# A fused attention and feed-forward kernel: another order of work up to the first MLP stage, quad 5's normalisation by a float32 product, and a planner that counts transfers as they run

## The chip, the cores and the metric

The kernel runs on one core of a Trainium2 chip. TensorE (PE) multiplies matrices into PSUM, which has eight banks; VectorE (DVE), ScalarE (ACT) and GpSimd (POOL) work on 128 partitions of SBUF; SyncE (SP) computes nothing and issues DMA transfers. SP, ACT and POOL each have a DMA queue of their own. Each engine runs its instructions in the order in which they were written for it, and waits on semaphores for the others. The metric is the device time of one execution in microseconds, lower is better.

## What is computed

Cosine attention over 8 batches of 12 heads, 448 positions and 64 dimensions, followed by a two-layer MLP over the 3584 tokens:

```python
q_n = q / (np.linalg.norm(q, axis=-1, keepdims=True) + 1e-06)
k_n = k / (np.linalg.norm(k, axis=-1, keepdims=True) + 1e-06)
scores = np.matmul(q_n, k_n.transpose(0, 1, 3, 2)) / tau          # tau = 0.1
attn = np.exp(scores - np.max(scores, axis=-1, keepdims=True))
attn = attn / (np.sum(attn, axis=-1, keepdims=True) + 1e-09)
x = np.matmul(attn, v).transpose(0, 2, 1, 3).reshape(3584, 768)
h = x @ w_in                                                      # 768 x 2048
out = (h * np.cos(h)) @ w_out                                     # 2048 x 768
```

## The kernel before

**Quads.** Attention runs over 24 quads of four heads each (three to a batch), and each quad over seven steps of 64 keys per head. Q and K are loaded in float32 (`load_one`, L398), squared (`square`, L448 and L450), summed (L454), turned into reciprocal norms (`inverse`, L480 to L493: logarithm and exponential on ACT, and for quads 1 to `FAST` = 7 a VectorE sum and reciprocal in place of the last two ACT steps) and scaled to bfloat16 (`scale`, L501). Then they are transposed: by PE for the first four quads (`transpose`, L523 and the copy at L534), by a transposing DMA on SP after that (`turn`, L544). A step's `scores` (L560) go to PSUM, one ACT exponential (L567) writes E, and `attend` (L577) adds E times V into banks 4 and 5.

**Sums and normalisation.** For quads 0 to 2 the sums of the exponentials are spread over all partitions by a product with ones (`spread`, L602) and inverted on ACT (L611, L612). From quad 3 on, `sums` (L645) makes them for one or two quads in one round with a narrow selector matrix: ACT inverts them (L652, L654) into Zs, SP writes Zs to a scratch tensor in DRAM (L655), two SP loads for each quad read it back spread over 64 partitions each (R, L661), and GpSimd (VectorE for quad 5) multiplies the saved product of E and V by R into xT (L665). Rounds before are [3], [4, 5], [6, 7] and so on.

**MLP.** For each batch c, 16 blocks of the first layer (`m1_part`, L679, 6 products each) run in 8 pairs, followed by ACT and VectorE steps for h cos h (`m1`, L697 to L703). The second layer (`m2`, L715) runs in tiles of 128 tokens and halves of 384 columns, 16 products each; VectorE copies a half out (L733) and SP stores it (L739). The first layer of batch 1 needs quads 3, 4 and 5, that of batch 2 needs quads 6, 7 and 8, and so on. W1 comes in four and W2 in four transfers on GpSimd's queue (L420, L425), V on the same queue (L410).

**Order.** Quads 0 to 2 are written out by hand, and under `P.strict` ACT, VectorE and GpSimd keep that order. Behind them a loop over the batches interleaves: while the second layer of batch c runs, quads of later batches do their scores and attend steps (five quads in c = 0: 3 to 7; then four, three, three, three, three). `group` writes two steps and `fill` the second-layer products between them; it also places the rounds that are due. PE always keeps the written order. For the other engines `Planner.pass_` simulates the program with booked durations and takes, for each engine, the ready operation with the earliest due time (`prio`: the time by which its reader on PE needs it, less a `lead`). `land` books DMA transfers: 1.2 us to the first byte, `moves` us of transfer, lengthened where another queue is active, 0.8 us to the semaphore:

```python
s = max(issued + self.FIRST, self.ring[ring])
...
self.ring[ring] = s + took
return self.ring[ring] + self.LAST
```

`warm` runs products on an identity matrix to keep PE busy at the start. Zs has two buffers, R two, the Q and K loads three each, V four.

Of the kernel before, what the change touches and what calls it, by code (L numbers as in the profile page):

```python
# [21 lines left out]
class Planner:  # L22
# [10 lines left out]
    FIRST, LAST = 1.2, 0.8  # L33
# [36 lines left out]
    def land(self, ring, issued, took):  # L70

        s = max(issued + self.FIRST, self.ring[ring])
        alone = took
        for other in self.ring:
            if other != ring:
                both = min(took, max(0.0, self.ring[other] - s))
                took += both
                if both:
                    self.ring[other] += min(both, alone)
        self.ring[ring] = s + took  # L80
        return self.ring[ring] + self.LAST

    PASSES, SPREAD = 0, 1.5

    def plan(self):

        rng = random.Random(1)
        shift = [0.0] * len(self.ops)
        least = max(o.end for o in self.pass_(shift))
        for _ in range(self.PASSES):  # L90
            n = rng.choice((8, 30, 100))
            i = rng.randrange(len(shift) - n)
            tried = list(shift)
            for k in range(i, i + n):
                tried[k] += rng.gauss(0.0, self.SPREAD)
            end = max(o.end for o in self.pass_(tried))
            if end <= least:
                least, shift = end, tried
        self.order = self.pass_(shift)
        return self.order  # L100

    def pass_(self, shift):
# [38 lines left out]
        self.ring = {"sp": 0.0, "pool": 0.0, "act": 0.0}  # L141
# [4 lines left out]
        while len(done) < len(ops):  # L146
            best = None
            for e in self.ENGINES:
# [16 lines left out]
                if best is None or s < best[0]:  # L165
                    best = (s, e, c)
            s, e, c = best
# [10 lines left out]
            o.end = self.land(e, avail[e], o.moves) if o.dma else s + o.dur + o.lat  # L178
            done.append(o)
            if c in queue:  # L180
                u = queue[c]
                left[u] -= 1
                if not left[u]:
                    pending[e].append(u)
            for u in users[c]:
# [86 lines left out]
def bass_cosine_attention__then__act_gcu_kernel(  # L272
# [49 lines left out]
    Zs = ring("Zs", 2, [128, S], F32)  # L322
# [34 lines left out]
    op("dve", 0.1, lambda e: e.memset(zeros, 0.0), w=["zeros", "iot"])  # L357

# [34 lines left out]
    def load_one(qd, w, part=ALL[0], after=(), eng="sp"):  # L393
# [5 lines left out]
                  w=cut(nm, s, part), dma=(nm, s, j0), moves=0.157 * (j1 - j0), after=after, keep=qd > 4)  # L399
# [7 lines left out]
    def load_v(qd, after=()):  # L407
# [3 lines left out]
                  w=[("V", s)], dma=("V", s), moves=1.34, after=after)  # L411
# [11 lines left out]
    def load_w2(i, hf):  # L423
        src = moe_w_out.rearrange("(f p) n -> p f n", p=128)[:, 8 * i:8 * i + 8, HW * hf:HW * hf + HW]
        return pool_dma(0.79, lambda e: e.dma_start(W2.ap()[:, 8 * i:8 * i + 8, HW * hf:HW * hf + HW], src),  # L425
                 w=[("W2", i, hf)], dma=("W2", i, hf), moves=4.14)

    H, NLEAD, FAST = 2 * NJ, 5.0, 7
# [110 lines left out]
    def turn(qd):  # L539
# [3 lines left out]
        for n, t, nm in ((Qn, qT, "Q"), (Kn, kT, "K")):  # L543
            turned[qd].append(op("sp", 1.3, lambda e, n=n, t=t: e.dma_start_transpose(  # L544
                t[u].ap().rearrange("p j a x -> p j (a x)"), n[u].ap().rearrange("p j r d -> p (j r d)")),
               r=cut(nm + "n", u, ALL[0]), w=cut(nm + "T", u, ALL[0]), dma=(nm + "T", u), moves=1.29, keep=True))
# [41 lines left out]
    Z, LEAD = 6, 15.0  # L588
# [44 lines left out]
    def sums(quads, bk):  # L633
# [3 lines left out]
        z = n % 2  # L637
# [17 lines left out]
        op("sp", 0.5, lambda e: e.dma_start(rscr.ap()[8 * n:8 * n + rows, :], Zs[z].ap()[0:32 * np_:16, :]),  # L655
           r=[("Zs", z)], w=[("rs", n)], dma=("rs", z), moves=0.05, lead=LEAD)
        for i, qd in enumerate(quads):
            u, sl, b = qd % 2, qd % NA, qd // QB
            for r in range(2):
                ap = bass.AP(rscr, (8 * n + 4 * i + 2 * r) * S, [[0, 64], [S, 2], [1, S]])  # L660
                op("sp", 0.5, lambda e, r=r, u=u, ap=ap: e.dma_start(R[u].ap()[64 * r:64 * r + 64], ap),  # L661
                   r=[("rs", n)], w=[("R", u, r)], after=spared, dma=("R", u, r), moves=0.68, lead=LEAD)
            c0 = 2 * (qd % QB)
            late = qd == 2 * QB - 1
            op("dve" if late else "pool", 1.02 if late else 2.04, lambda e, u=u, sl=sl, b=b, c0=c0: e.tensor_tensor(  # L665
                xT[b % 2].ap()[:, c0:c0 + 2, :], AVs[sl].ap(), R[u].ap(), ALU.mult),
                r=[("AV", sl), ("R", u, 0), ("R", u, 1)], w=[("x", b % 2, qd % QB)], lead=LEAD)

# [40 lines left out]
    def m2(t, h, f0, f1, bk):  # L709
# [11 lines left out]
        if f1 == NNB and t == B * S // 128 - 1:  # L721
# [3 lines left out]
            for sg, eng in enumerate(("sp", "act" if h else "sp")):  # L725
# [4 lines left out]
                   r=[("o", so, h)], w=[("out", t, sg, h)], dma=("store", t, h, sg), moves=0.26)  # L730
# [82 lines left out]
    for _ in key:  # L813
        pass
# [226 lines left out]
```

## Time and profile before

| | us |
|---|---|
| median of 3 runs (lowest, highest) | 438.72 (436.95, 439.27) |
| the profiled execution's own time | 440.37 |
| its span | 438.6 |
| first exponential of quad 0 starts | 12.32 |
| first layer of batch 0 starts (L679) | 37.09 |
| quads 3 to 7 with the second layer of batch 0 | 60.30 to 95.95 |
| first layer of batch 1 starts | 98.72 |
| mean granted PE clock | 0.995 |

The span is the time between the first and the last instruction of one profiled execution; the time of that execution has another 1.8 us around it. A line of the profile's timeline gives start, duration, engine, source line, operation, the tile written and the tiles read, and in brackets how long the engine idled before it and what ended that. In the table of stretches each engine has its busy time and number of instructions, then come the granted PE clock, the share of the DMA engines and GB/s. The chain of waits is followed back from the last instruction.

### The profile page before, as it was taken

The numbers are of one execution on the slowest core, as the hardware profiler recorded it, in microseconds if no ns is written. First come the engines' busy times: TensorE is split into PE (matmuls) and PEld (weight loads), VectorE is DVE, ScalarE is ACT, GpSimd is POOL, SyncE is SP. The second block draws the span as 40 slices with busy tenths as digits, with TensorE's granted clock in tenths as the row PEclk, the third lists the DMA queues.
The fourth block names the chain that finished last, engine by engine and source line by source line (L and its number), as shares of the span: only waits on it lengthen the run. The fifth ranks groups of instructions, "written<-read, shape, count | busy, mean of one in ns | idle before, by whom it ended". The sixth has DMA issues, their size and how long they took to land.

```text
span 438.6 us, 8468 instructions
## 1 busy us (share of the span) xinstructions
PE 420.0 (96%) x3578; PEld 208.9 (48%) x3578; DVE 256.1 (58%) x316; ACT 311.5 (71%) x448; POOL 211.4 (48%) x145
## 2 busy tenths in 40 slices
PE   8889999979999999999999899998999999999996
PEld 7344543324544445444554354443454445565563
DVE  4866995346963539823895329923495225925931
ACT  4898889984888777798688557887678757704800
POOL 3887636858157893379526683157642033000000
PEclk9999999998999999999999999999999999999999
DMA  7999997998519997187934994067951614021023
GB/s 255 235 255 223 271 195 125 220 242 157 153 44 232 231 206 193 37 217 107 263 100 85 225 240 123 0 148 159 209 100 37 152 51 122 1 72 37 0 66 80
DMA packets 70943, 64.35 MB, mean 147 GB/s; under 512 B 40100, under 2 KB 63224, under 8 KB 70904
## 3 DMA queue, kind: packets, MB, share of 16 engines
q1 hardware_dynamic: 57992, 51.45, 46.9%
q0 software_dynamic: 12288, 11.80, 17.8%
q8 instruction: 28, 0.46, 0.4%
q10 hardware_dynamic: 624, 0.56, 0.4%
q14 instruction: 11, 0.09, 0.1%
HBM read 55.25 MB, written 11.16 MB: 151 GB/s over the span
## 4 chain that ended last, share of the span: by engine, by line
PE 80%; ACT 6%; DVE 4%; DMA 4%; issue 2%; POOL 2%; SPq 0%; POOLq 0%
PE PS L679 33%; PE PS L715 29%; PE PS L560 7%; PE PS L577 6%; ACT E L567 4%; PE PS L645 3%; DMA Qf<-in_q_dram 2%; DVE n L454 1%; DMA rscr<-Zs 1%; DMA R<-rscr 1%; DVE gT L703 1%; DVE osb L733 1%; DVE ar L698 0%; POOL xT L665 0%; PE PS L602 0%
## 5 line engine op out<-in xcount | busy, mean ns | idle before, releaser
L715 PE MATMUL PS<-W,gT 128*128 128x384 bf16 x896 | 161.9, 327 | 0.1
L567 ACT ACTIVATE E<-PS 128x896 bf16<-128x896 f32 x168 | 144.7, 915 | 23.8 <-PE PS L560 22.0
L679 PE MATMUL PS<-xT,W 128*128 128x448 bf16 x768 | 149.4, 355 | 2.8 <-POOL xT L665 2.8
L715 PEld LDWEIGHTS PS<-W,gT 128*128 128x128 bf16 x896 | 80.8, 98 | 77.7 <-issue 28.2
L679 PEld LDWEIGHTS PS<-xT,W 128*128 128x128 bf16 x768 | 74.8, 98 | 74.9 <-issue 3.5
L697 ACT ACTIVATE ar<-PS 128x896 int32<-128x896 f32 (+1 forms) x72 | 58.7, 827 | 48.7 <-PE PS L679 48.7
L698 DVE SCALAR_TENSOR_TENSOR ar<-ar,PS 128x896 f32<-128x896 int32 (+1 forms) x72 | 69.2, 978 | 28.2 <-ACT ar L697 28.1
L733 DVE COPY osb<-PS 128x384 f32<-128x384 f32 x54 | 30.1, 557 | 74.5 <-PE PS L715 73.4
L703 DVE TENSOR_TENSOR gT<-PS,ar 128x896 bf16<-128x896 f32 (+1 forms) x72 | 69.5, 983 | 1.4 <-ACT ar L700 1.0
L700 ACT ACTIVATE ar<-ar 128x896 f32<-128x896 f32 (+1 forms) x72 | 60.7, 862 | 12.5 <-DVE ar L698 11.8
L560 PE MATMUL PS<-qT,kT 64*64 64x448 bf16 x672 | 61.2, 362 | 5.2 <-issue 1.8
L450 POOL TENSOR_TENSOR sqq<-Qf 128x896 bf16<-128x896 f32 x21 | 35.2, 1677 | 58.5 <-DVE n L454 42.3
L665 POOL TENSOR_TENSOR xT<-AVs,R 128x896 bf16<-128x896 f32 x20 | 41.5, 2084 | 43.5 <-DMA R<-rscr 43.4
L577 PE MATMUL PS<-E,Vb 64*64 64x448 bf16 x672 | 48.9, 352 | 2.4 <-DVE AVs L586 1.7
L450 POOL TENSOR_TENSOR sqk<-Kf 128x896 bf16<-128x896 f32 (+1 forms) x22 | 36.5, 1657 | 28.4 <-DVE n L454 18.6
L501 POOL TENSOR_TENSOR Qn<-Qf,rr 128x896 bf16<-128x896 f32 x21 | 36.2, 1726 | 17.9 <-ACT rr L493 17.5
L586 DVE COPY AVs<-PS 128x896 f32<-128x896 f32 x21 | 22.9, 1091 | 34.3 <-PE PS L577 34.3
L501 POOL TENSOR_TENSOR Kn<-Kf,rr 128x896 bf16<-128x896 f32 (+1 forms) x22 | 36.6, 1665 | 0.5 <-DVE Qn L501 0.5
L560 PEld LDWEIGHTS PS<-qT,kT 64*64 64x64 bf16 x672 | 18.6, 104 | 37.2 <-issue 14.4
L454 DVE TENSOR_REDUCE n<-sqq 128x14 f32<-128x896 bf16 (+2 forms) x24 | 24.9, 1038 | 10.9 <-POOL sqq L450 10.8
L454 DVE TENSOR_REDUCE n<-sqk 128x14 f32<-128x896 bf16 (+2 forms) x24 | 25.0, 1042 | 6.9 <-POOL sqk L450 6.9
L577 PEld LDWEIGHTS PS<-E,Vb 64*64 64x64 bf16 x672 | 19.2, 106 | 16.5 <-ACT E L567 6.7
(53 smaller groups left out, 176.4 us busy)
## 6 DMA issues: line engine op xcount, KB each, us to landing
Qf<-in_q_dram SPq DMA_DIRECT2D x24, 448.0 KB, 5.8
out_dram<-osb SPq DMA_DIRECT2D x54, 192.0 KB, 3.6
Kf<-in_k_dram SPq DMA_DIRECT2D x23, 448.0 KB, 6.3
R<-rscr SPq DMA_DIRECT2D x42, 224.0 KB, 4.4
Vb<-in_v_dram POOLq DMA_DIRECT2D x24, 224.0 KB, 5.7
W<-in_moe_w_in_dram POOLq DMA_DIRECT2D x4, 768.0 KB, 18.4
W<-in_moe_w_out_dram POOLq DMA_DIRECT2D x4, 768.0 KB, 32.3
Kf<-in_k_dram ACTq DMA_DIRECT2D x1, 320.0 KB, 6.2
```

What stands on the lines that cost most here:

```text
L450: op(eng, (1.68 if eng == "pool" else 1.05) * n, lambda e: e.tensor_tensor(dst, src, src, ALU.mult), r=cut(nm + "f", s, part), w=at, after ...
L454: return op("dve", 0.07 + 0.95 * n, lambda e: e.tensor_reduce(out=n2[u].ap()[:, H * w:H * w + H] if part == ALL[0] else jr(n2[u], w, part) ...
L501: lambda e: e.tensor_tensor(n[u].ap()[:, j0:j1].rearrange("p j r d -> p r j d"), f[s].ap()[:, :, j0:j1], rb, ALU.mult),
L560: ins = e.matmul(bank(bs + r, S, 64 * a, 64 * a + 64), kT[u].ap()[64 * r:64 * r + 64, j, a, :], qT[u].ap()[64 * r:64 * r + 64, :, a, :], s ...
L567: act("exp", 0.875, lambda e: e.activation(E[es].ap(), two(bs), ACT.Exp, bias=0.0, scale=INV_TAU), r=pair(bs), w=[("E", es)], chain="E")
L577: ins = e.matmul(bank((X, Y)[a], S, 64 * r, 64 * r + 64), Vb[vs].ap()[64 * a:64 * a + 64, r, j, :], E[es].ap()[64 * a:64 * a + 64, r, :], ...
L679: ins = e.matmul(bank(bk + i2), W1.ap()[:, i, 128 * nb:128 * nb + 128], xT[c % 2].ap()[:, i, :], start=(i == 0), stop=(i == NKC - 1))
L697: op("act", 0.195 + 0.31 * n, lambda e: e.activation(ai, src, ACT.Identity, bias=0.25, scale=INV2PI), r=bs, w=at)
L698: op("dve", 0.06 + 0.47 * n, lambda e: e.scalar_tensor_tensor(a, ai, -2.0 * math.pi, src, ALU.mult, ALU.add), r=bs + at, w=at)
L700: act("sin", 0.22 + 0.32 * n, lambda e: e.activation(a, a, ACT.Sin, bias=GUARD * math.pi / 2.0, scale=GUARD), r=at, w=at)
L703: op("dve", 0.07 + 0.47 * n, lambda e: e.tensor_tensor(gT.ap()[:, f0:f1, col:col + S], src, a, ALU.mult), r=bs + at, w=[("g", c % 2, f) fo ...
L715: ins = e.matmul(bank(bk, HW), gT.ap()[:, f, col:col + 128], W2.ap()[:, f, HW * h:HW * h + HW], start=(f == 0), stop=(f == NNB - 1))
```

## The change

The planner books a transfer as a flow: `land` is replaced by `flow`, in which the queues' first transfers share the engines, by 1.0 for SP and ACT and 1.6 for GpSimd, with a loss of 1.11 for each further active queue; the first byte takes 0.6 us and the semaphore 1.0. The durations booked for transfers are new, and eleven fixed shifts (`LEADS`) are added to the due times of runs of operations. Leads fall from 15 to 5 (sums) and from 5.0 to 2 (norms), and `FAST` covers all quads.

Rounds become [3, 4], [5], [6, 7] and so on. Quad 5's reciprocals are not sent through DRAM: two float32 products with a selector `selB` spread them over a PSUM bank, each followed by a VectorE multiply into half of its xT. `fill` places rounds and these products by a due position among the second layer's products, at blocks 4 to 12 of a tile.

In the written order of quads 0 to 2, all of quad 0's K is loaded on SP behind Q, its longer part is squared on ACT, the steps of Q's and K's norms alternate, one K copy moves to ACT, the square of quad 1's K goes to GpSimd, its norm runs apart from Q's, and the W1 and V loads come later in GpSimd's order. Quad 3 is transposed before the last six products of the first layer of batch 0, no longer behind them.

```diff
-    FIRST, LAST = 1.2, 0.8
+    FIRST, LAST, CROWD = 0.6, 1.0, 1.11
+    SHARE = {"sp": 1.0, "act": 1.0, "pool": 1.6}
...
-    def land(self, ring, issued, took):
...
+    def flow(self, until):
+
+        while True:
+            on = [r for r, q in self.ring.items() if q and q[0][1] <= self.now]
+            if on:
+                part = len(on) / (1.0 + self.CROWD * (len(on) - 1)) / sum(self.SHARE[r] for r in on)
+            at, which = until - self.LAST, None
+            for r, q in self.ring.items():
+                if q:
+                    t = self.now + q[0][2] / (part * self.SHARE[r]) if r in on else q[0][1]
+                    if t <= at:
+                        at, which = t, r
...
+                o.end = at + self.LAST
+                return o
...
+    LEADS = (
+        (603, 20, -9.5),
+        (1176, 20, 9.3),
...
     def plan(self):
...
+        for i, n, by in self.LEADS:
             for k in range(i, i + n):
-                tried[k] += rng.gauss(0.0, self.SPREAD)
...
+                shift[k] += by
         self.order = self.pass_(shift)
...
-    Zs = ring("Zs", 2, [128, S], F32)
+    Zs = ring("Zs", 1, [128, S], F32)
+    selB = sb("selB", [128, 2, 128], F32)
...
-                  w=cut(nm, s, part), dma=(nm, s, j0), moves=0.157 * (j1 - j0), after=after, keep=qd > 4)
+                  w=cut(nm, s, part), dma=(nm, s, j0), moves=0.19 * (j1 - j0), after=after, keep=qd > 4)
...
-    H, NLEAD, FAST = 2 * NJ, 5.0, 7
+    H, NLEAD, FAST = 2 * NJ, 2, NQ
...
-    Z, LEAD = 6, 15.0
+    Z, LEAD = 6, 5
...
+        if quads == [2 * QB - 1]:
+            return [lambda bk, a=a: spread_out(quads[0], a, bk) for a in range(2)]
...
-            late = qd == 2 * QB - 1
-            op("dve" if late else "pool", 1.02 if late else 2.04, lambda e, u=u, sl=sl, b=b, c0=c0: e.tensor_tensor(
+            op("pool", 2.04, lambda e, u=u, sl=sl, b=b, c0=c0: e.tensor_tensor(
...
+    def spread_out(qd, a, bk):
+        sl, b, c0 = qd % NA, qd // QB, 2 * (qd % QB)
+        op("pe", 0.76, lambda e: e.matmul(bank(bk), selB.ap()[0:64, a, :], Zs[0].ap()[0:64, :], start=True, stop=True),
+           r=[("Zs", 0), "selB"], w=whole(bk), mode="b")
+        op("dve", 0.57, lambda e: e.tensor_tensor(xT[b % 2].ap()[:, c0 + a, :], AVs[sl].ap()[:, a, :], bank(bk), ALU.mult),
+           r=[("AV", sl)] + whole(bk), w=[("x", b % 2, qd % QB)], lead=LEAD)
...
-    ROUNDS = [[FIRST]] + [[i, i + 1] for i in range(FIRST + 1, NQ, 2)]
-    E1, E2 = NNB - 6, NNB - 4
+    ROUNDS = [[FIRST, FIRST + 1], [FIRST + 2]] + [[i, i + 1] for i in range(FIRST + 3, NQ, 2)]
+    E1, E2, SLO, SHI = NNB - 6, NNB - 4, 4, 12
...
     for part in KP:
-        load_one(0, 1, part, eng="act")
+        load_one(0, 1, part)
...
-    square(0, 1, "dve", KP[0])()
-    key = inverse(0, 1, 2, KP[0])
...
-    adds.append(square(0, 1, "pool", KP[1]))
...
+    first = square(0, 1, "dve", KP[0])
+    adds = [square(0, 0, "act", part) for part in QP]
+    rest = square(0, 1, "act", KP[1])
     adds[0]()
-    warm(24)
+    warm(6)
     warm(WARM, 1)
     adds[1]()
...
+    first()
+    rest()
+    chains = inverse(0, 0, 1), inverse(0, 1, 2, KP[0])
+    for _ in range(4):
+        for x in chains:
+            next(x, None)
+    for _ in inverse(0, 1, 2, KP[1]):
+        pass
     scale(0, 0, "dve", QP[0])
     warm(5)
+    scale(0, 1, "dve", KP[0])
     scaled = scale(0, 0, "dve", QP[1])
-    transpose(0, 1, 7, KP[0])
+    adds = [square(1, 0, "act")]
     transpose(0, 0, 6, QP[0])
+    transpose(0, 1, 7, KP[0], eng="act")
     transpose(0, 0, X, QP[1])
+    load_v(0, gate[:1])
+    load_v(1)
     scale(0, 1, "pool", KP[1], after=[scaled])
-    adds = [square(1, w, "act") for w in range(2)]
-    for i in range(2):
-        load_w1(0, i)
-    load_v(2)
-    for i in range(2):
-        load_w1(1, i)
+    adds.append(square(1, 1, "pool"))
     adds[0]()
-    adds[1]()
     load_qk(3)
+    query = inverse(1, 0, 1)
...
+                for _ in query:
+                    pass
+                adds[1]()
+                scale(1, 0, "dve")
+                squares = [square(2, 0, "pool")]
+                for i in range(2):
+                    load_w1(0, i)
+                load_v(2)
...
+                    squares.append(square(2, 1, "pool", after=[scaled]))
+                    for i in range(2):
+                        load_w1(1, i)
                     load_v(3)
...
+            if c == 0 and pr == NNB // 2 - 1:
+                m1_part(c, pr, at_bank[pr], (0,), 0, NKC)
+                transpose(FIRST, 0, free)
+                transpose(FIRST, 1, free + 1)
+                m1_part(c, pr, at_bank[pr], (1,), 0, NKC)
...
+        def can_sum(p):
+            return max(due[0][0], 2 * NNB) <= p < len(items) and SLO <= items[p][2] <= SHI
+
         def fill(n):
+            while due and due[0][0] <= at[0] + n and len(banks) == 2 and at[0] + n < len(items) and not any(map(can_sum, range(at[0], at[0] + n))):
+                n += 1
...
-                elif due and len(bank_of) != 1 and at[0] >= 2 * NNB and 2 <= f0 <= 13:
-                    sums(due.pop(0), 13 - cur[0])
+                elif due and can_sum(at[0]):
+                    what = due.pop(0)[1]
+                    more = (what if callable(what) else lambda bk: sums(what, bk))(13 - cur[0])
+                    due.extend((at[0] + 3 + 3 * i, x) for i, x in enumerate(more or ()))
```

More of the change, by code (lines that the diff above doesn't have):

```diff
@@ L166, in pass_ @@
                     best = (s, e, c)
+            landed = self.flow(best[0] if best else 1e9) if flying else None
+            if landed:
+                flying -= 1
+                for u in users[landed.i]:
+                    ue = ops[u].eng
+                    ready_at[u] = max(ready_at[u], landed.end + self.HOP[ue])
+                    left[u] -= 1
+                    if not left[u] and ue != "pe":
+                        pending[ue].append(u)
+                continue
             s, e, c = best
@@ L1002, in bass_cosine_attention__then__act_gcu_kernel @@
             flush_av()
[L1003 removed]
+            due.extend((0, r) for r in ROUNDS if r[-1] == NQ - 1)
         fill(len(items))
+        for _, what in [x for x in due if callable(x[1])]:
+            what(13 - cur[0])
+        due[:] = [x for x in due if not callable(x[1])]
     P.emit(nc, ctx)
```

118 lines of the change are left out of this document (59 added, 59 removed).

## The prediction

> **What bounds the kernel now.** The page comes first, for the span and the engines' shares.
>
> ```profile
> span 438.6 us, 8468 instructions
> ...
> PE 420.0 (96%) x3578; PEld 208.9 (48%) x3578; DVE 256.1 (58%) x316; ACT 311.5 (71%) x448; POOL 211.4 (48%) x145
> ...
> PE 80%; ACT 6%; DVE 4%; DMA 4%; issue 2%; POOL 2%; SPq 0%; POOLq 0%
> ```
>
> TensorE sets the time, but a share over the whole span hides where it does not. So the second view is the busy time by stretch: quads 3 to 7 (60.30 to 95.95), the wait behind them, and the second first-layer stage cut at the changes of the clock.
>
> ```profile
> 60.30:95.95 35.65, 34.59 (x386) 12.53 (x384) 18.37 (x26) 32.53 (x46) 24.84 (x17) 1.00 1.00 200
> 95.95:98.72 2.77, 0.01 (x1) 0.01 (x1) 0.94 (x2) 2.42 (x8) 2.12 (x2) 1.00 0.82 125
> ...
> 99.25:102.67 3.42, 3.42 (x11) 1.37 (x9) 0.83 (x2) 0.11 (x1) 3.42 (x2) 0.50 0.34 74
> ```
>
> In the first row PE is busy 34.59 of 35.65 us and ACT 32.53: both are nearly full, so neither has much room for more. In the second PE does nothing. In the third the granted clock is 0.50. The chain of waits says what PE waited for:
>
> ```profile
> 82.61 1.47 PE PS L645 x28
> 84.10 0.55 ACT Zs L652
> 84.68 0.58 ACT Zs L654
> 85.26 1.27 ACT E L567 x2
> 86.53 4.74 DMA rscr<-Zs
> ...
> 91.80 4.72 DMA R<-rscr
> 96.60 2.07 POOL xT L665
> 98.72 6.40 PE PS L679 x24
> ```
>
> The row sums of quads 4 and 5 leave PE at 84.1. Their reciprocals go to DRAM and back in two transfers of 4.7 us, and GpSimd multiplies quad 4 until 98.67. The 24 products behind take 6.40 us; the same 24 take 4.54 at 157.94. Third, the waits of PE after 119 us:
>
> ```profile
> PE PS L560 <- issue: 1.8, 1, 1.8
> PE PS L577 <- DVE AVs L586: 1.7, 1, 1.7
> PE PS L645 <- DVE osb L733: 0.9, 1, 0.9
> ```
>
> Last, the start, by timeline:
>
> ```profile
> 4.75 0.63 ACT L448 ACTIVATE sqq<-Qf 128x512 bf16<-128x512 f32 x1 [1.66 <-DMA Qf<-in_q_dram]
> 7.56 1.25 POOL L450 TENSOR_TENSOR sqk<-Kf 128x640 bf16<-128x640 f32 x1 [6.49 <-DMA Kf<-in_k_dram]
> 9.58 1.15 DVE L501 TENSOR_TENSOR Qn<-Qf,rr 128x512 bf16<-128x512 f32 x2
> 11.89 0.57 PE L560 MATMUL PS<-qT,kT 64*64 64x448 bf16 x8 [0.61 <-DVE qT L534]
> ```
>
> The first exponential is at 12.32, and from there to 37 us ACT has little idle time (0.28 before its third exponential, 0.45, 0.69, 0.81). What brings that first exponential forward brings the first-layer stage forward.
>
> **The sum's base.** The profiled execution took 440.37 us, 1.65 over the median of 438.72. The terms are taken off 440.37, and 1.65 goes off at the end.
>
> **A, the start.** All of quad 0's K now goes through SP's queue behind Q, instead of ACT's queue beside it. Loads that have the queue to themselves land about 1.2 us apart (K of quad 1 at 8.10, Q and K of quad 2 at 9.31 and 10.46, 448 KB each). Counting back at that pace, Q of quad 0 lands at 4.6 (4.73 now), the short K piece at 4.9 (as now), the long one at 5.8 instead of 7.49. Its square moves from GpSimd (1.25) to ACT (about 0.7 by L448's 0.51 to 0.63), so it ends at 6.5 instead of 8.8. VectorE then runs the sums: Q to 6.7, K to 7.9 (reductions of 1.32, 0.42 and 0.82). ACT interleaves eight short steps at 0.245 us each, Q's last ending at 8.6. Three scalings (0.63, 0.42, 0.51) end at 10.2; the last Qn now ends at 10.73. With the same 1.2 us of transposing and copying behind it the first scores come at 11.1, and the first exponential at 11.5: 0.8 earlier. In between ACT does one kT copy (about 0.34) but only one square of quad 1, not two (0.93 each). The second kT copy waited on VectorE behind two reductions of 1.07 and 1.08 (it runs at 13.74); behind one it comes at about 12.3, so the 0.28 before ACT's third exponential goes too. A is -1.1.
> What is moved past what: on GpSimd's queue the square of quad 1's K and one of quad 2's (1.7 each) stand ahead of the first two W1 issues, which go from 12.1 to about 14.7; the other two, behind a square that waits for K of quad 1 to be scaled, from 14.2 to about 19; W2 stays near 21. These are paid with cover: the first W1 pieces landed at 21.2 and 28.0 and are wanted at about 36, the last at 39.6 and wanted at about 44; the transfers are busy anyway until 14.0 with V (issued earlier, at 7) and until 17.0 with quad 3. If that cover is gone, the stage waits by what they are late. Bounds: -1.9 (all four ACT gaps too) to +0.3 (ACT's added copy uncovered).
>
> **B, quad 5.** Quads 3 and 4 now share a round, a quad earlier than quad 4 had it; quad 5 has its own, its reciprocals spread by two float32 products into PSUM, and VectorE multiplies from there. Rounds stay two (1.50 us with 14 or 28 matmuls alike). Gone: the wait of 2.78, and the half clock, 3.41 x 0.5 = 1.7. Added on PE: no row has a float32 product; it lies between one bfloat16 pass of that width (0.19) and a whole round (1.50). I take the 0.76 that the diff books, between the two: 1.5 for both. Four changes of array layout at the planner's 0.115: 0.5. The added wait: ACT's two steps end 1.2 us after the round (84.08 to 85.26), and PE reaches the product three second-layer matmuls later (0.5): a wait of 0 to 0.7, I take 0.3. Queued behind it on PE are the scores of quads 6 and 7, for which ACT waits. Sum 2.3, of which 0.5 fits into the 1.06 us that PE idles in that stretch: +1.8. VectorE's two half multiplies (0.55 each) replace one of 1.57, and have cover (18.37 busy of 35.65); two R loads go from SP. B is -4.5 + 1.8 = -2.7. Bounds: -4.5 (0.19 each, all absorbed) to +0.4 (1.5 each, 0.5, two waits of 0.7).
> The clock: here PE idled 2.78 us and ran at half clock 0.5 us after it resumed; waits of 1.75 and less were followed by no such stretch. The Trainium skill ("TensorE: Matmul & The Clock Gate", What's actually happening) has the clock fall after at least one whole idle window of about 3.4 us. By that rule 2.78 would be too short, the 1.7 would not hang on this wait, and B would be -1.0; the row decides for me. For the product the skill ("FP8 and Floating Point Precision", TensorE Precision Notes) states four passes; as an estimate from it, 4 x 0.19 = 0.76 and the same sum.
>
> **C, the planner.** It decides the order on every queue. It booked a Q load alone at 1.2 + 1.1 + 0.8 = 3.1 us; measured is a median of 5.8, and 8.1 where the wait of 1.69 arose at 251.24: VectorE's reduction of that load stood ahead of the copy that PE needed. The new booking, with GpSimd's queue active, is 0.6 + 1.33/0.365 + 1.0 = 5.2 (0.365 is 2/2.11 over 2.6). I count that wait as gone, -1.7. The 0.88 before a round at 142.93 shrinks as rounds start two matmuls later into a tile: -0.35. The 1.75 before 300.09 is a turned K that landed at 300.00; I leave it. Against that, eleven shifts and lower leads reorder all queues: one new wait like the smallest, +0.9. C is -1.2; bounds -4.3 (all three gone) and +4.5 (one more wait like 98.72's with its clock).
> FAST over all quads takes two ACT steps (0.23) from 16 quads and gives VectorE 0.54 each. Nothing: from 119.20 to 162.98 ACT is busy 35.06 of 43.78 us and VectorE 20.81; with that cover gone it would cost up to 8.6. Turning quad 3 before the last six products of its stage moves PE work without adding any: nothing, within a microsecond either way.
>
> Sum: 440.37 - 1.1 - 2.7 - 1.2 = 435.4, less 1.65: **433.7**.
>
> **Rivals.**
> Slower: the later rounds' reciprocals come late. Their lead falls from 15 to 5, so other work on ACT, SP and GpSimd may go ahead. The round at 142.93 reaches its xT at 156.43, a chain of 13.5; its readers start at 162.92, so it decides from 6.5 us longer. At 264.04 the margin is 10.1. With 12 us more (less than two quads' norms on GpSimd, 4 x 1.68 each) PE waits 5.5 + 1.7 and 1.9: 442.8. Against it: due times still order the queues.
> The same: TensorE becomes the bound in quads 3 to 7; B at +0.4 and C at 0 give 440.37 - 0.7 - 1.65 = 438.0. For it: 34.59 busy of 35.65.
> Faster by less: W or turned K is late. K of quad 4 landed at 66.0 and was read at 67.3, so a start 1.1 earlier nearly meets it; A goes, 434.8.
> The clock stays low though the wait is gone, the page's case: 433.7 + 1.7 = 435.4.
>
> **The numbers.** Forecast 0.47, its own range 430.5 to 436.5; late transfers 0.08; clock 0.04; PE-bound 0.18; late reciprocals 0.23. Half a per cent (2.2 us) is about what a measurement can tell from no change: faster is below 436.5, slower above 440.9. Faster 0.58, same 0.18, slower 0.24, a sliver of the first cases crossing over. The bounds add to -10.7 and +5.2, 428.0 to 443.9; all at one end is unlikely, so 428.5 to 443.5.
>
> **What would show it.** A: the first exponential near 11.5 and the first L679 row near 36. B: no wait before the second L679 stage, clock 1.00 through it, two products of about 0.76. C: no wait of AVs readers near 250. Wrong: a wait of L679 for xT at any later stage, PE waiting for Zs, or a first-layer stage waiting for W.

## The result, and the profile after

| | before | after |
|---|---|---|
| median of 7 runs, us (lowest, highest) | 439.45 (436.95, 444.67) | 433.80 (431.61, 436.63) |
| profiled execution, us | 440.37 | 433.80 |
| its span | 438.6 | 431.5 |
| first exponential of quad 0 | 12.32 | 10.76 |
| first layer of batch 0 starts | 37.09 | 34.90 |
| first layer of batch 1 starts | 98.72 | 98.38 |
| first layer of batch 2 starts | 157.78 | 154.93 |
| first layer of batch 4 starts | 259.09 | 253.85 |
| first layer of batch 5 starts | 309.10 | 302.08 |

After to before is 0.9876, with an interval of 0.9828 to 0.9924: in this measurement the kernel became about 5.5 us faster. In two later groups of runs, with 23 runs of the old kernel in each, it came out some 7 to 8 us faster (ratios 0.9812 and 0.9836 below). The number forecast was 433.7. The ratios leave out disturbed executions, and as the profiled execution of one run below (the old start) was disturbed, that run is read by its times alone.

Lines of the changed kernel are numbered differently: L594 is the scores (L560 before), L601 the exponential (L567), L611 attend (L577), L679 the row sums (L645), L700 the multiply by R (L665), L706 and L708 the new float32 product and its multiply, L721 the first layer (L679), L757 the second (L715). The page of the changed kernel, span, engines and shares of the chain:

```profile
span 431.5 us, 8448 instructions
...
PE 419.4 (97%) x3564; PEld 208.5 (48%) x3564; DVE 264.7 (61%) x351; ACT 305.9 (71%) x419; POOL 211.3 (49%) x146
...
PE 80%; DMA 9%; ACT 3%; POOL 3%; SPq 2%; DVE 1%; issue 0%; POOLq 0%
```

PE has as much work as before (419.4 against 420.0); what went is its idle time. In the chain, DMA rose from 4% to 9%: what is still waited for is a transfer. The table of stretches says where it is (columns as before: length, busy time of PE, PEld, DVE, ACT, POOL, the granted PE clock, DMA share, GB/s):

```profile
34.90:98.38 63.48, 60.65 (x532) 25.99 (x529) 39.77 (x54) 52.38 (x74) 40.40 (x27) 0.97 1.10 205
...
67.43:70.84 3.41, 3.41 (x23) 1.14 (x21) 1.92 (x3) 2.88 (x4) 2.36 (x2) 0.50 0.60 110
...
98.38:154.93 56.55, 56.52 (x502) 26.82 (x500) 36.23 (x48) 44.66 (x62) 37.26 (x25) 1.00 0.76 174
```

From batch 0's first layer to batch 1's the kernel takes 63.48 us where the old one took 61.63, and the half clock that stood behind 98.72 now stands at 67.43. From batch 1's first layer on, PE idles 0.03 us in 56.55, at clock 1.00, where it idled 1.03 in 59.06 at 0.97. The chain of waits, at the place in question:

```profile
46.54 5.36 SPq L578
...
51.95 14.46 DMA kT<-Kn
...
66.45 0.38 PE PS L594 x4
```

The turned K of quad 4 takes 14.46 us from its issue to its landing at 66.41, and PE goes on at 66.45. The waits of PE from 20 us on (total, times, longest):

```profile
PE PS L594 <- DMA kT<-Kn: 1.9, 1, 1.9
PE PS L594 <- ACT E L601: 1.8, 5, 0.5
```

That turned K is the only single wait of 1 us or more that is left. The waits of 0.88, 1.69 and 1.75 at 142.93, 251.24 and 300.09, and that of 2.78 at 98.72, are all gone. The timeline of the start, and of quad 5's two products:

```profile
6.27 0.74 ACT L482 ACTIVATE sqk<-Kf 128x640 bf16<-128x640 f32 x1 [0.92 <-DMA Kf<-in_k_dram]
6.91 0.29 ACT L514 ACTIVATE nrm<-n 128x14 f32<-128x14 f32 x2
...
7.64 0.31 ACT L527 ACTIVATE rr<-nrm 128x14 f32<-128x14 f32 x2
...
10.33 0.57 PE L594 MATMUL PS<-qT,kT 64*64 64x448 bf16 x8 [0.54 <-DVE qT L568]
...
82.90 1.50 PE L679 MATMUL PS<-E,sel 128*32 128x448 bf16 x14
...
85.81 1.02 PE L706 MATMUL PS<-Zs,selB 64*128 64x448 f32 x2
86.76 0.66 PE L757 MATMUL PS<-W,gT 128*128 128x384 bf16 x3
...
89.78 1.02 PE L706 MATMUL PS<-Zs,selB 64*128 64x448 f32 x2 [0.18 <-DVE osb L775]
```

The long K piece lands at 6.25 (its square follows at 6.27), the first scores are at 10.33 (11.89 before). A product is a group of two matmul instructions, and the next work starts 0.95 us after it began: the change of layout is in that. The first waits for nothing, the second 0.18 for a free bank.

### The profile page after: what moved, and what is told of

Read it like the earlier page. It is cut to its first block, busy times and chain, and to the rows that moved or that the text cites. A ratio compares the mean times of both kernels' runs of the same rounds, so it can differ in the third digit from the quotient of the medians.

```text
span 431.5 us, 8448 instructions
## 1 busy us (share of the span) xinstructions
PE 419.4 (97%) x3564; PEld 208.5 (48%) x3564; DVE 264.7 (61%) x351; ACT 305.9 (71%) x419; POOL 211.3 (49%) x146
## 4 chain that ended last, share of the span: by engine, by line
PE 80%; DMA 9%; ACT 3%; POOL 3%; SPq 2%; DVE 1%; issue 0%; POOLq 0%
PE PS L757 33%; PE PS L721 30%; PE PS L594 8%; PE PS L611 6%; DMA Kf<-in_k_dram 4%; DMA kT<-Kn 3%; PE PS L679 3%; ACT E L601 3%; DMA Qf<-in_q_dram 2%; SPq L578 2%; POOL Qn L535 1%; POOL sqk L484 1%; POOL Kn L535 1%; SPq L432 1%; DVE Qn L535 0%
## 5 line engine op out<-in xcount | busy, mean ns | idle before, releaser
L601 ACT ACTIVATE E<-PS 128x896 bf16<-128x896 f32 x168 | 144.7, 915 | 28.7 <-PE PS L594 27.7
L757 PE MATMUL PS<-W,gT 128*128 128x384 bf16 x896 | 163.0, 328 | 0.1
L721 PE MATMUL PS<-xT,W 128*128 128x448 bf16 x768 | 147.7, 353 | 0.0
L757 PEld LDWEIGHTS PS<-W,gT 128*128 128x128 bf16 x896 | 80.9, 98 | 79.5 <-issue 29.3
L721 PEld LDWEIGHTS PS<-xT,W 128*128 128x128 bf16 x768 | 74.5, 98 | 70.2 <-issue 1.5
L594 PE MATMUL PS<-qT,kT 64*64 64x448 bf16 x672 | 61.7, 365 | 4.9 <-DMA kT<-Kn 1.9
L700 POOL TENSOR_TENSOR xT<-AVs,R 128x896 bf16<-128x896 f32 x20 | 41.5, 2085 | 36.1 <-DMA R<-rscr 35.8
L535 POOL TENSOR_TENSOR Qn<-Qf,rr 128x896 bf16<-128x896 f32 x21 | 35.3, 1685 | 30.1 <-DVE rr L523 30.0
L611 PE MATMUL PS<-E,Vb 64*64 64x448 bf16 x672 | 48.4, 354 | 0.4
L484 POOL TENSOR_TENSOR sqk<-Kf 128x896 bf16<-128x896 f32 x22 | 36.9, 1676 | 19.8 <-DVE n L488 17.4
L594 PEld LDWEIGHTS PS<-qT,kT 64*64 64x64 bf16 x672 | 18.8, 105 | 37.9 <-issue 13.9
L444 POOL DMA_DIRECT2D Vb<-in_v_dram x24 | 18.1, 756 | 18.9 <-PE PS L594 12.6
```

Source lines behind the costliest of these rows:

```text
L484: op(eng, (1.68 if eng == "pool" else 1.05) * n, lambda e: e.tensor_tensor(dst, src, src, ALU.mult), r=cut(nm + "f", s, part), w=at, after ...
L535: lambda e: e.tensor_tensor(n[u].ap()[:, j0:j1].rearrange("p j r d -> p r j d"), f[s].ap()[:, :, j0:j1], rb, ALU.mult),
L594: ins = e.matmul(bank(bs + r, S, 64 * a, 64 * a + 64), kT[u].ap()[64 * r:64 * r + 64, j, a, :], qT[u].ap()[64 * r:64 * r + 64, :, a, :], s ...
L601: act("exp", 0.875, lambda e: e.activation(E[es].ap(), two(bs), ACT.Exp, bias=0.0, scale=INV_TAU), r=pair(bs), w=[("E", es)], chain="E")
L611: ins = e.matmul(bank((X, Y)[a], S, 64 * r, 64 * r + 64), Vb[vs].ap()[64 * a:64 * a + 64, r, j, :], E[es].ap()[64 * a:64 * a + 64, r, :], ...
L721: ins = e.matmul(bank(bk + i2), W1.ap()[:, i, 128 * nb:128 * nb + 128], xT[c % 2].ap()[:, i, :], start=(i == 0), stop=(i == NKC - 1))
```

## The experiments

The parts were taken out one at a time, put into the old kernel one at a time, and the one wait that was left was attacked in three ways. Comparisons are ratios to the old kernel on the same chip; the changed kernel itself stands in this table three times.

| kernel | median, us | ratio (interval) |
|---|---|---|
| changed kernel, first measurement | 433.80 | 0.9876 (0.9828, 0.9924) |
| changed kernel, with the 2nd group of runs | 431.84 | 0.9812 (0.9747, 0.9877) |
| changed kernel, with the 3rd group | 432.88 | 0.9836 (0.9806, 0.9865) |
| 1st group: quad 4 turned before quad 7 is loaded | 435.62 | 0.9893 (0.9845, 0.9942) |
| 1st group: quad 5 through DRAM | 437.06 | 0.9908 (0.9873, 0.9943) |
| 1st group: old start | 435.96 | 0.9893 (0.9860, 0.9926) |
| 1st group: no shifts | 434.60 | 0.9897 (0.9841, 0.9952) |
| 2nd group: ten shifts | 433.39 | 0.9865 (0.9808, 0.9921) |
| 2nd group: old planner | 436.92 | 0.9938 (0.9900, 0.9976) |
| 2nd group: old kernel, new planner only | 444.65 | 1.0084 (1.0051, 1.0117) |
| 3rd group: quad 4 transposed on PE | 431.13 | 0.9795 (0.9768, 0.9821) |
| 3rd group: old kernel, new start only | 439.28 | 0.9948 (0.9910, 0.9985) |
| 3rd group: old kernel, product only | 439.71 | 0.9977 (0.9949, 1.0005) |

**Quad 5 through DRAM.** The product goes, quad 5 takes the transfers and the VectorE multiply of before; start, rounds and planner stay, and the shifts keep their operations.

```diff
-        if quads == [2 * QB - 1]:
-            return [lambda bk, a=a: spread_out(quads[0], a, bk) for a in range(2)]
...
-            op("pool", 2.04, lambda e, ...
+            late = qd == 2 * QB - 1
+            op("dve" if late else "pool", 1.02 if late else 2.04, lambda e, ...
```

> The changed kernel, with quad 5's reciprocals sent through DRAM again and multiplied on VectorE, in its own round as in the change; the shifts keep to their operations. Theory: the second first-layer stage waits for quad 5's xT, 3 us or more, with half clock behind it, less the 1.9 us of PE time that the two products take: 2 to 5 us slower than the changed kernel, 436 to 439. Rival: with quad 5 in a round of its own and the new order the trip through DRAM would be hidden, so that the product is only PE time: 0 to 2 us faster than the changed kernel.

It took 437.06, the ratio 0.9908. PE waits twice at batch 1's first layer, first for GpSimd's multiply, then for VectorE's of quad 5:

```profile
96.91 1.69 PE L720 MATMUL PS<-xT,W 128*128 128x448 bf16 x8 [1.27 <-POOL xT L699]
101.14 3.20 PE L720 MATMUL PS<-xT,W 128*128 128x448 bf16 x16 [2.55 <-DVE xT L699]
```

The two waits come to 3.8 us, where the product costs 1.9 us of PE. In this execution the clock stayed at 1.00 behind them. Its span of 433.0 lies 1.9 to 3.6 above those executions of the changed kernel, in other groups of runs, that also kept the clock at 1.00 (429.4 to 431.1). So the product is worth having inside the changed kernel, and what it is worth there fits the forecast's B (2.7).

**The old start.** Everything else as changed, the shifts re-indexed.

```diff
-        load_one(0, 1, part)
+        load_one(0, 1, part, eng="act")
...
-    chains = inverse(0, 0, 1), inverse(0, 1, 2, KP[0])
-    for _ in range(4):
-        for x in chains:
-            next(x, None)
...
+    adds.append(square(0, 1, "pool", KP[1]))
```

> The changed kernel, with the written order of quads 0 to 2 of before (K beside Q on ACT's queue, W1 early, and so on); the shifts keep to their operations. The first-layer stage of batch 0 starts near 37.1 in place of 34.9. Theory: quad 4's turned K bounds the stretch behind it, so the 2.2 us are mostly not passed on: the wait for K shrinks or goes, the second first-layer stage starts at 98.4 to 99.5, and the time is 0 to 1 us more than the changed kernel's, 434 to 435. Rival: the gain of the start is passed on in full: 436.

Measured: 435.96, ratio 0.9893. By the ratios that is 0.2 to 0.8 per cent above the changed kernel, whose first interval it overlaps. The spans say more: in executions that kept the clock at 1.00 they are 432.0 to 433.5, against 429.4 to 431.1 for the changed kernel (in other groups of runs). So the theory that the turned K had eaten nearly the whole gain of the start is not borne out: 1 to 4 us come through, and the rival's 2.2 lies among them. What this kernel itself waits for stays open, as its trace is not read.

**No shifts.** `LEADS` is emptied.

```diff
-    LEADS = ( ... eleven shifts ... )
+    LEADS = ()
```

> The changed kernel without the eleven shifts of due times, all else the same. Theory: the waits of before at 142.9, 251.2 and 300.1 (4.3 us together) went because transfers are booked at about what they take, so they stay away without the shifts, and the time is 0 to 1.5 us more than the changed kernel's. Rival: the shifts took them away by hand; then two of them or others like them come back, 2 to 5 us more.

434.60, ratio 0.9897, whose interval overlaps the changed kernel's; the spans at clock 1.00 are 432.3 to 432.6, some 1 to 3 us above those of the changed kernel. The old waits at 251 and 300 stay away, so the shifts are not needed for that. Of the 0.88 before a round at 142.93, 0.55 is left here (at 138.59), and none in the kernels with shifts. The shifts also matter in the first batch. Here quad 6's K is issued 3.7 us earlier, and quad 4's turn with it. The row below is the issue of quad 6's K on SP in this kernel (45.09 in the changed one):

```profile
41.43 0.37 SPq L420 DMA_DIRECT2D Kf<-in_k_dram  x1
```

Quad 4's turned K lands at 64.09 instead of 66.41, and PE doesn't wait for it. In exchange PE waits 1.46 at 55.50 (second layer) and 1.75 at 156.54 (first layer, for GpSimd's xT). The row of the first names VectorE, but the second of W2's four pieces lands at 55.41 (52.22 in the changed kernel), 0.09 before PE goes on. One shift of the eleven (-21.6, on eight operations) lets GpSimd scale quad 3's K after all of quad 4; quad 6's K waits for that buffer. That pointed to it as the cause of the wait at 66.

**Ten shifts.** That one shift alone is dropped.

```diff
-        (221, 8, -21.6),
```

> The changed kernel less one of its eleven shifts, the one that puts quad 4's scalings and turning transfers 21.6 us ahead of their due time. Without any shifts GpSimd scaled quad 3 whole before quad 4, the load of quad 6's K went out at 41.43 and not at 45.09, and quad 4's K landed at 64.09 and not at 66.41. Theory: that one shift makes the wait of 1.9 us, as it holds SP's queue behind a load that waits for quad 3's K; without it there is no wait near 66, the second first-layer stage starts near 96.2 in place of 98.4, and the time is 1.5 to 3.5 us less than the changed kernel's. Rival: the wait only moves to the next turned K or to the multiplies of quads 3 and 4, and the time changes by less than 1 us.

433.39, against 431.84 for the changed kernel in the same group. Quad 4's K lands at 64.28 and isn't waited for, but the second layer of batch 0 is:

```profile
57.71 2.72 PE L756 MATMUL PS<-W,gT 128*128 128x384 bf16 x8 [3.60 <-DVE qT L567]
```

The row names a VectorE copy, which had ended at 57.26; the second of W2's four pieces landed at 57.62, again 0.09 before PE goes on. The loads of quad 6's K and quad 7's Q are issued 3.4 and 2.2 us earlier and W2 lands 5.4 us later. The same piece ends a wait in three more kernels: no shifts, and below the old planner and the start alone (landings at 55.78 and 55.39). In all four quad 6's K is issued by 41.7; in the other traces that are read it is issued at 43.9 or later, and the piece has landed by 52.6. That the one makes the other is still a reading of the lists of transfers and was not tried by itself. The wait only moves, as the rival said; this execution took 437.88, the longest of its six, so not every one need wait 3.60.

**Quad 4 turned before quad 7 is loaded.** One line changes its place.

```diff
     norm_b(FIRST + 1, after=ended[-1:])
-    load_qk(FIRST + 4)
     turn(FIRST + 1)
+    load_qk(FIRST + 4)
```

> The changed kernel, with the two turning transfers of quad 4 written ahead of the Q and K loads of quad 7 on SP's queue, no longer behind them. Theory: quad 4's turned K, which landed at 66.41 where its first score could have run at 64.5, is what hands back the start's gain. Then the wait of 1.90 us and the half clock behind it go: K lands near 62, the second first-layer stage starts near 95 to 96.5, and the time falls by 1.5 to 3.6 us against the changed kernel (433.8), to 430 to 432. Rival: the stretch of quads 3 to 7 is full on PE and ACT anyway, or the GpSimd multiplies of quads 3 and 4, which ended at 98.18, only 0.2 us before the stage at 98.38, set its start; then the wait goes but the stage still starts at 97.5 or later, and the time changes by less than 1 us apart from the clock.

435.62: not faster. Quad 4's K lands at 61.78 and its wait is gone, but PE now waits for quad 5's. GpSimd shows why, and PE the price:

```profile
64.25 1.68 POOL L484 TENSOR_TENSOR sqq<-Qf 128x896 bf16<-128x896 f32 x1 [10.57 <-DMA Qf<-in_q_dram]
```

```profile
74.73 0.38 PE L594 MATMUL PS<-qT,kT 64*64 64x448 bf16 x4 [2.83 <-DMA kT<-Kn]
```

In GpSimd's order the square of quad 7's Q stands ahead of quad 5's scaling. The load of quad 7 was issued later, so GpSimd stood 10.57 us at that square, the scaling came at 68.44 instead of 63.47, and quad 5's turned K landed at 74.69. With the two runs on the shifts, this makes three orders in which a wait for one transfer became a wait for another. From 20 to 66 us the DMA share is 1.1 to 1.3 in the changed kernel (0.70 from 66 to 75), and these orders only chose who is late.

**Quad 4 transposed on PE.** So the next try takes transfers away. Quad 4 isn't turned by DMA; PE transposes its Q and K in two groups of seven into a bank that is free there, inside the second layer of batch 0.

```diff
-    due = []
+    due, TURN = [], (2 * NNB, 2 * NNB + 4)
...
-    turn(FIRST + 1)
+    due.extend((p, lambda bk, w=w: transpose(FIRST + 1, w, bk)) for w, p in enumerate(TURN))
...
-            fill(2 * (NNB - E2) + 3 * len(due) if i == 0 else ...
+            fill(2 * (NNB - E2) + 3 * len(due) * (c > 0) if i == 0 else ...
```

> The changed kernel, with quad 4's Q and K transposed on PE into the idle one of the two second-layer banks (two matmul groups of about 0.5 us, two VectorE copies of 0.6) in place of the two turning transfers; the shifts keep to their operations. Theory: the DMA queues are full up to about 66 us and quad 4's turned K is the last thing that the stretch waits for; with it off the queues the wait of 1.5 to 1.9 us goes, the second first-layer stage starts 0.5 to 1.5 us earlier, and the time is 0.5 to 2.5 us less than the changed kernel's on the same chip. Rival: PE and ACT are full in that stretch, and the added 1 us on PE or another late transfer takes the place of the wait: the same within 0.5 us, or more.

431.13 (430.90 to 431.88), beside 432.88 (432.15 to 434.46) for the changed kernel in the same group: the two ranges don't meet. Its page and its whole list of PE's waits between 26 and 380 us:

```profile
span 429.2 us, 8470 instructions
...
PE 419.3 (98%) x3578; PEld 209.1 (49%) x3578; DVE 265.4 (62%) x353; ACT 306.0 (71%) x419; POOL 211.4 (49%) x146
...
PE 87%; ACT 7%; DMA 2%; issue 1%; DVE 1%; POOL 1%; SPq 0%; POOLq 0%
```

```profile
PE PS L594 <- ACT E L601: 0.4, 2, 0.2
PE PS L721 <- POOL xT L700: 0.3, 1, 0.3
PE PS L611 <- ACT E L601: 0.2, 1, 0.2
PE PS L636 <- ACT ar L645: 0.2, 1, 0.2
```

Fourteen transposes of 0.06 us each at their pace (0.39 for seven) cost PE about 0.8, and VectorE two copies of 0.61; the 1.5 to 1.9 of waiting, and the half clock that followed it in some executions, are gone. This version beats both kernels, by 2.05 per cent and by 0.4. The half clock is not the whole of it: at clock 1.00 its spans are 428.8 to 429.8, those of the changed kernel in this group 429.9 to 431.1.

**The changed kernel again**, beside the other kernels of the second and third group.

> The changed kernel unchanged, as the measure for the others on the same chip: 433 to 436 us, with the wait of about 1.9 us for quad 4's turned K near 66, and none after 100.

> The changed kernel unchanged, as the measure for the others on the same chip: 431.5 to 434.5 us, with the wait of 1.5 to 1.9 us for quad 4's turned K near 66.

431.84 and 432.88. The wait for quad 4's turned K is there both times, 1.54 at 65.80 in the first and 1.80 at 66.50 in the second; a half clock follows the second only.

**The old planner.** New start and product, but the old booking, leads and `FAST`, and no shifts.

```diff
-    def flow(self, until): ...
+    def land(self, ring, issued, took): ...
...
-    H, NLEAD, FAST = 2 * NJ, 2, NQ
+    H, NLEAD, FAST = 2 * NJ, 5.0, 7
...
-    Z, LEAD = 6, 5
+    Z, LEAD = 6, 15.0
```

> The changed kernel with before's planner: its booking of transfers and their durations, no shifts, the old leads and FAST for seven quads; the new written order of the start and quad 5's product stay. Theory: the three waits after 119 us (0.9, 1.7, 1.8), or as many like them, come back, 2 to 4.5 us over the changed kernel. Rival: the planner is worth nothing of itself and the start and the product bring the whole gain: within 1 us of the changed kernel.

436.92, which is 5.1 above the changed kernel in the same group. Its waits are 1.67 at 55.87 (W2's second piece), 2.41 at 93.03 (a turned K), 0.56 at 142.43 and 1.76 at 297.45 (a turned K). The old wait at 251 is not among them. The first and the third stand in the new planner without shifts too (1.46 and 0.55), so it is the shifts that take these two away.

**The planner alone.** The old kernel with the new booking, leads and `FAST`, without shifts.

> The kernel before with the new planner alone: transfers booked as flows with the new durations, the new leads, FAST for all quads, no shifts; the old start and quad 5 through DRAM. Theory: the waits near 251 and 300 go and the one before the second first-layer stage stays: 1.5 to 3.5 us under the kernel before. Rival: without the start and the product the planner brings nothing, or its lower leads bring later waits for xT: the same or up to 3 us more than before.

444.65, slower than before by 0.5 to 1.2 per cent, the only kernel that is. The old waits near 251 and 300 are gone. But at batch 1's first layer, where quads 4 and 5 still share a round and go through DRAM, PE waits 4.36 for GpSimd's xT at 101.06 and 1.08 at 105.30 for VectorE's, and the clock is at one half from 98.84 to 109.08. The chain of waits there:

```profile
87.28 5.17 DMA rscr<-Zs
...
94.26 7.00 DMA R<-rscr
...
101.28 3.97 DVE xT L682
```

The read of the reciprocals takes 7.00 us where it took 4.72. That is the forecast's slower rival at another place: reciprocals that go through DRAM come late. That other loads ahead of them make it so is a reading, not shown. Three more waits stand behind it: 0.88 at 148.05 before a round, 1.59 at 156.84 for a turned K and 1.56 at 167.92 for GpSimd's xT.

**The start alone and the product alone**, each in the old kernel.

> The kernel before with the new written order of quads 0 to 2 and the earlier turning of quad 3 alone; the old planner and quad 5 through DRAM. The first-layer stage of batch 0 starts 2 us earlier, near 35. Theory: the gain is handed on at most in part, as the second first-layer stage waits for xT and quad 4's K on the full DMA queues: 0.3 to 2 us under the kernel before. Rival: it is handed on in full, 2.2 us or more.

> The kernel before with quad 5's product, its rounds and its places in the second layer alone; the old start and the old planner. Theory: the wait of 2.8 us before the second first-layer stage goes, for 1.9 us of products on PE, and the half clock behind that wait with it: 1 to 3 us under the kernel before. Rival: PE is full there, and what the product adds eats what the wait gave: within 0.7 us of the kernel before.

439.28 (ratio 0.9948) and 439.71 (0.9977). With the start alone, batch 0's first layer begins at 34.40 instead of 37.09, but batch 1's at 101.17 instead of 98.72:

```profile
101.17 5.07 PE L679 MATMUL PS<-xT,W 128*128 128x448 bf16 x17 [2.95 <-POOL xT L665]
```

In this execution (441.54) the 2.7 us won are spent in waits of 1.96 at 55.48, 2.27 at 82.82 and this one, with two stretches of half clock. Over all runs part of the gain comes through (ratio 0.9948). With the product alone quad 5 is ready by 91, and PE waits for a turned K instead:

```profile
93.79 0.38 PE L566 MATMUL PS<-qT,kT 64*64 64x448 bf16 x4 [1.92 <-DMA kT<-Kn]
```

Half clock follows it, and batch 1's first layer starts at 100.62. By the ratios, the start alone is worth 2.3 us, the product 1.0 (its interval reaches past 1, so that alone it can't be told from no change), and the planner costs 3.7; start and product together are worth 2.7, all three 8.3 (both in the second group). The planner needs the other two: alone it loses, behind them it brings over 5. In each of these traces a wait that goes leaves another.

## Why the prediction was right, and where it was not

The number was right to 0.1 us and the direction too; its terms were not. In the two profiled executions the start gained, a wait in the first batch took more than that back, the product gave what was forecast and a little more, and the planner gave four times its term.

| term | forecast | measured in the profiles | how |
|---|---|---|---|
| A, the start | -1.1 | -2.2 | first layer of batch 0 from 37.09 to 34.90 |
| turned K of quad 4 late | in a rival | +3.6 | wait 1.90, half clock 3.41 x 0.5 = 1.7 |
| B, quad 5 | -2.7 | -3.4 | -1.7 by 98.38 (all of -0.34 less the two rows above), -1.7 of clock behind it |
| C, the planner | -1.2 | -5.1 | the rest of -7.1 |
| sum | -5.0 | -7.1 | span 438.6 to 431.5 |

The table splits by place: A up to batch 0's first layer, the turned K and B up to batch 1's with its half clock, C all that is behind.

**Base.** The forecast for the profiled execution was 435.4, and it took 433.8. Its span fell by 7.1 and its time by 6.6, as the time around the span grew from 1.8 to 2.3. The 1.65 that was taken off to come to the median belongs to the execution of before. The kernel became 5.5 us faster, and 5.0 was forecast: the two agree through errors of 2.5 us (A with the turned K) and 3.9 (C) that largely cancel. That the number was met to 0.1 us is luck twice over: by the ratios of the two later groups the change is worth 8.3 and 7.2 us.

**A** was mis-sized, past its bound of -1.9. The landings came as worked out or nearly: 4.28, 4.69 and 6.25 for Q, short and long K (forecast 4.6, 4.9 and 5.8). The step that failed is "eight short steps at 0.245 us each, Q's last ending at 8.6". Written alternately from two independent chains, they ran in pairs: a pair every 0.25 us, 1.04 for all eight (6.91 to 7.95). That is most of why the first exponential came at 10.76 and not at 11.5. It is 1.6 earlier than before; the other 0.6 of A was won between it and 34.90.

**Late transfers** were the rival with 0.08, as "K of quad 4 landed at 66.0 and was read at 67.3, so a start 1.1 earlier nearly meets it". Its mechanism is the one that happened, and the margin was read rightly: a start earlier by 2.2 reached the transfer before it landed, at 66.41. What it left out is the half clock behind the wait. It was given as a case that excludes the forecast, and the total came out all the same, because C covered it.

**B** held in its parts. Gone are the wait of 2.78 and the 1.7 of clock, and batch 1 starts at clock 1.00. Two products cost 1.9 with their changes of layout (forecast 1.5 + 0.5), the waits 0.2 (forecast 0.3). The parts make -2.4; the 1.0 beyond them stands in no row of the product. From batch 0's first layer to batch 1's, PE's small gaps shrink from 1.13 to 0.75, and its busy time grows by 2.93 where half clock and products account for 3.6, with 528 other matmuls beside 529. Where those 0.7 went stays open. The margin is thin: GpSimd's last multiply for batch 1 ends at 98.18 and its first product runs at 98.38. The Trainium skill ("FP8 and Floating Point Precision", TensorE Precision Notes) states four passes for true float32; the estimate from that page, 0.76, is the price taken, and the trace's 0.95 with the layout's change is near it, in two instructions.

**C** was mis-sized. All three waits went, 4.3 together, where 1.7 + 0.35 were counted; the wait that the forecast left, before 300.09, went as well. The "one new wait like the smallest, +0.9" of the reordering is the turned K, if one likes, whose wait is made by a shift that delays quad 6's load. What is over, 0.8 us, is in stretches without a named wait: 154.93 to 202.75 is 0.49 shorter than its counterpart. Three ways led there. The 0.88 went as forecast at first: with the new places of the rounds 0.55 or 0.56 is left (product alone, old planner, no shifts), the planner alone keeps 0.88, and only the kernels with shifts have none. The waits near 251 and 300 are missing in every trace with the new booking that is read, with shifts or without, so the booking with its leads is enough to remove them; which of its constants does it was not tried. It is not the only way: the old kernel with the new start alone has neither of them (it waits 1.09 at 268.15), and the old planner in the changed kernel has only the one near 300.

**The other rivals.** PE did not become the bound in quads 3 to 7. The clock did not stay low behind the gone wait: at 98.38 it is 1.00. Late reciprocals, the slower rival, did not occur in the changed kernel (its longest wait for xT is 0.5, in the third group), but are real: the planner alone runs into them at the first place where reciprocals go through DRAM with a short margin, and is slower than before.

## What to carry to other kernels

Ask, before summing up what each part gains, which transfer is next behind each wait that goes: with the product alone a turned K came next and the gain can't be told from none, and with the planner alone late reciprocals turned it into a loss. Where the queues are full for tens of microseconds, as here from 20 to 66, three reorderings moved the wait from one transfer to another (quad 4's, quad 5's, W2's); taking transfers out of the queue removed it, even at the price of 0.8 us on the busiest engine. Before believing the engine that a row names for a wait, compare when it ended with when the operands' transfers landed. A sum whose total comes out right is no evidence for its terms: check each by its own row.

## What the runs showed of the hardware

**Half clock after short waits.** A stretch of half clock measured 3.41 us, or three times that (10.24, around the wait of 4.36). In the profiled executions it followed single waits of 1.80, 1.90, 1.92, 2.27, 2.41, 2.78, 2.83, 2.95 and 3.60 us, beginning between 0 and 1.3 us after PE resumed, and did not follow 1.54, 1.69, 1.75, 1.96, 2.45 and 2.55. So between 1.8 and 2.6 the length of the wait alone does not decide it, and the forecast's line at 1.75 was too sharp. Its place in time does most of the rest. In every trace the time from one change of the clock to the next is a whole multiple of 3.413 us (in the changed kernel 61.44, which is 18 times that, up to the half clock at 67.43), so each execution can be cut into windows of that length. Up to the last matmul there are ten windows behind which the clock fell to one half, and PE idled 1.80 to 3.41 us in each; in the windows behind which it stayed at 1.00 PE idled at most 1.76, but for one with 1.96 (start alone). The waits of 2.45 and 2.55 lie across a border, with at most 1.37 and 1.73 in one window. The changed kernel's spans fall accordingly: 429.4 to 431.1 where the granted clock is 1.00 for the whole execution, 431.2 to 432.2 where it is 0.996, about one stretch. The Trainium skill ("TensorE: Matmul & The Clock Gate", What's actually happening) has the half clock after at least one idle window of some 3.4 us, and the window running free of the kernel. The length of 3.41 agrees, and so does the running free: in the three profiled executions of the changed kernel borders lie at 67.43, 67.31 and 68.04 (the last counted on from where its clock record begins). That a whole window must be idle does not agree, since 1.80 us in one was enough.

**A transposing transfer in full queues.** Quad 4's K took 14.46 us to land, quad 5's, issued at 67.20 when the queues had emptied (DMA share 0.70 from 66 to 75), 3.04. Its issue held SP for 4.92 and 1.30 us in turn, so what stood behind it on SP's queue was issued that much later. On PE the same transpose is seven matmuls in 0.39 us, with a VectorE copy of 0.61.

**Two chains in one engine.** Steps on ACT that depend on each other came every 0.245 us (7.10, 7.35, 7.59 and 7.84 in the old start); alternated between two independent chains, two came in 0.25.
